# Expert sums closed and added in three regions, the last expert's addition between its halves, 60 of 72 conversion pieces among the experts

## The chip, the cores and the metric

One core of one Trainium2 chip runs the whole program in one launch. The metric is the device time in microseconds (us) of one execution. Engines are named as in the profile: PE (TensorE), DVE (VectorE), ACT (ScalarE), POOL (GpSimd), SP (SyncE, which here only issues DMAs).

## What is computed

Sparse attention over 4 x 576 tokens gives x with 2304 rows of 512. Then two stages follow, cut here to what the change touches:

```python
P = sinkhorn(exp(x @ w_gate - max))            # 2304 x 8
out = 0
for e in range(8):                             # 8 experts, hidden size 1024
    h = np.maximum(x @ w1[e], 0.0)
    out += P[:, e:e + 1] * (h @ w2[e])
xn = out / sqrt(mean(out * out) + 1e-6) * rms_g
g = xn @ w_gate; val = xn @ w_val              # 512 x 1536
return (g / (1 + exp(-g)) * val) @ w_out       # 1536 x 512
```

The weights `w_gate`, `w_val` and `w_out` of the last stage come as 64-bit numbers and are made into 32-bit numbers by integer arithmetic on DVE.

## The kernel before, in words

**Tiling.** The 2304 tokens lie in three thirds `qd` of six tiles of 128. A third is used as a 2 x 2 block matrix: tiles 0 to 2 are the upper half, tiles 3 to 5 the lower (`half`), and the 512 columns are two blocks of 256 (`col`). Every matrix product is taken in a scheme of seven block products instead of eight, and every factor is split into a high and a low part, so that one block product is three matmuls for each of two chunks: `product` (L1151) issues six matmuls of 128x384 into the PSUM buffer `ub`.

**Order of work.** After attention, expert 0 is done in a plain way. Experts 1 to 7 are 42 *groups* n = 0 to 41: for each expert, its hidden half `hh` 0 over the three thirds (0, 1, 2), then half 1 over (2, 1, 0). A group has 14 *slots*; in each, one `product` of the first layer is issued and then one `unit` (L1752, nine matmuls of 128x256 into the PSUM buffer `db`) of the second layer, which belongs to the slot 12 earlier (`LAG`). So the last units of an expert run in the next expert's first group, n = 6k. Every second unit completes one of seven second-layer products k = 0 to 6, and `evict_1(n, k)` takes it from `db` into `acc`, the third's output sums: for k = 0, 2, 3, 4 of hidden half 0 by a copy on ACT (L1773), otherwise by an addition on DVE (L1775, 768 columns, or 1536 for k = 5). First-layer outcomes in `ub` are copied by ACT (L1294), put through a ReLU by ACT (L1298, L1302), or added on DVE (L1183).

**Closing an expert.** After k = 5 and k = 6 of hidden half 1, one half of a third is complete. `weigh` multiplies it by the router's P in place on ACT (three times L1788), and `gather` sends it by an adding DMA of POOL's queue to `y1d` in DRAM (L1796). The next expert begins with the third that the last one ended with, so its copy L1773 must wait until that DMA has read `acc`. For the last expert the DMA goes the other way, `acc += y1d` (L1798), and the normalization of that half waits for it.

**Normalization.** `norm_scale` takes the mean square of a tile (ACT, POOL) and scales it (`xn`, L1393 on DVE). `turn_tile` transposes the tile on PE (L1403) into `db` and multiplies it on DVE by `rms_g` back into `acc`. `norm_blocks` makes the block sums and their high and low parts (L1420 on ACT; L1421 on DVE or, for two thirds of the tokens, on POOL) and stores them to `xnd` in DRAM by SP's queue (L1430, L1454), from where `load_block` (L1083) brings the seven input blocks of a third into `xt` and `xx`. Three blocks are *plain*, four are sums.

**The last stage.** `passes`: three column ranges p, each over the three thirds, n = 0 to 8, and two halves j a pass, written p0.0, p0.1, p1.0 and so on. A half pass has 14 steps, each with one `product` (seven for `w_gate`, seven for `w_val`), and 12 output products of the half pass before are issued between them. p0.0 has the last 12 units of the experts in their place.

**What sets the order.** No scheduler moves instructions: they are issued as the code is run. A `Background` clock `bg` is pumped twice a slot; `bg.add(steps, slots)` spreads steps over pumps, a `Queue` holds steps with lags in pumps, and `drain(tag)` issues at once all that is left of a tag. The 72 *conversion pieces* (`conversion`, seven DVE operations L831 to L855, a load and a store each) are such a queue `conv`; 48 are begun at group 5 and 24 at pass 1, with a lag `CONV_WAIT` ahead of each.

Of the kernel before, what the change touches and what calls it, by code (L numbers as in the profile page):

```python
# [8 lines left out]
F32 = mybir.dt.float32  # L9
F32R = mybir.dt.float32r  # L10
# [103 lines left out]
def kernel(  # L114
# [1262 lines left out]
    def norm_scale(qd, t0):  # L1377

        ss, junk = cv[:, 1280 + t0 : 1283 + t0], cv[:, 768:1280]
# [18 lines left out]
        steps = [(1, lambda t=t: sq(t)) for t in range(3)] + [(1, mean), (0, root)]  # L1398
        return steps + [(2 if t == 0 else 0, lambda t=t: xn(t)) for t in range(3)]
# [10 lines left out]
    def norm_blocks(qd, i, spare, close):  # L1410
# [34 lines left out]
        def part(k):  # L1445
            src = (b12, tb, ta, b21)[k]
            parts(src, highs[k // 2][:, 256 * (k % 2) : 256 * (k % 2 + 1)], src.bitcast(F32R), nc.gpsimd if close else nc.vector)
            return 0 if close else 256
# [10 lines left out]
        steps = [plain, add1, keep, add2] + [lambda k=k: part(k) for k in range(4)] + [keep2]  # L1459
        return [(0.85 if close else 1.2, f) for f in steps]  # L1460


    with tc.manual_schedule():
# [263 lines left out]
        norm = Queue(bg)  # L1727
        turns = {}
# [32 lines left out]
        def evict_1(n, k):  # L1761
# [21 lines left out]
            if hh == 1 and k >= 5:  # L1783
                half = k - 5

                def weigh(m):
                    b = 3 * half + m
                    nc.scalar.activation(  # L1788
                        acc[:, qd, b], acc[:, qd, b], AF.Copy, scale=prob[:, tile_of(qd, b), g : g + 1]
                    )  # L1790

                def gather():
                    t, y = acc[:, qd, 3 * half : 3 * half + 3], y1d[:, qd, half]
                    if g < E - 1:
                        bg.drain("first")
                        nc.gpsimd.dma_start(out=y, in_=t, accum_op=ALU.add)  # L1796
                    else:
                        nc.gpsimd.dma_start(out=t, in_=y, accum_op=ALU.add)  # L1798
                        norm.add([(SUM_WAIT, lambda: None)] + norm_scale(qd, 3 * half), ("scale", qd, half))

                bg.add([lambda m=m: weigh(m) for m in range(3)] + [gather], 4, bg.now + 1, ("expert", qd))

        def turn_tile(qd, t, ps, spare, close):
            bg.drain(("expert", qd))
            norm.drain(("scale", qd, t // 3))
            norm_turn(ps, qd, t)
            if t >= 3:
                norm.add(norm_blocks(qd, t - 3, spare, close), ("blocks", qd))
# [12 lines left out]
        for n in (NGP - 3, NGP - 2):  # L1821
            for at, tiles in TURN_AT:
                turns[14 * n + at] = [(n, t) for t in tiles]
# [10 lines left out]
        def second(slot):  # L1834
# [13 lines left out]
            for m, t in turns.get(slot, ()):  # L1848
                if m not in spares:
                    spares[m] = spare_of(m)  # L1850
                turn_tile(groups[m][2], t, db[5], spares[m], True)
# [23 lines left out]
        halves = {}  # L1875
# [69 lines left out]
        for k in ready:  # L1945
            load_block(nmap[k], *to, k)
# [165 lines left out]
```

## Time and profile before

| what | value |
|---|---|
| time, median of 3 runs | 2287.49 us (2285.51 to 2291.5) |
| profiled execution | 2289.84 us, of which its span is 2288.0 us |
| PE busy | 2066.1 us, 90% of the span |
| DVE busy | 1663.8 us, 73% |
| ACT busy | 1175.6 us, 51% |
| POOL busy | 178.0 us, 8% |
| DMA traffic | 391.20 MB, mean 171 GB/s |

PE is busy nine tenths of the span, and the rest is idle time in certain places. A row of windows gives for a stretch of the span its length and each engine's busy time with its instructions, then the granted TensorE clock as a share of full speed, and the DMA engines' share and rate. A row of waits says which PE work stood still for which operation of which engine or DMA.

### The profile page before, as it was taken

To read this page: it belongs to the slowest core of one execution; us is meant where nothing else is said; L and a number is where in the kernel's file an instruction comes from. 1 tells how busy PE (TensorE), PEld (TensorE's weight loads), DVE (VectorE), ACT (ScalarE), POOL (GpSimd) and SP (SyncE) were. 2 spreads that over 40 slices of the span, in tenths; PEclk is the share of its full clock that TensorE was granted. 3 is DMA by queue.
4 is the path that set the end of the run, shared out by engine and by line. 5 is a ranking of instruction groups with operands and counts; after the bars stand their busy time and mean duration, and the time that the engine had idled before them with its cause. 6 is when DMAs were issued, how large, how long until landed. Compare 5 with 4: busy or idle time off the path is not lost. (4 is left out here: it accounts for less than half of the span.)

```text
span 2288.0 us, 37002 instructions
## 1 busy us (share of the span) xinstructions
PE 2066.1 (90%) x13611; PEld 1961.8 (86%) x13611; DVE 1663.8 (73%) x3553; ACT 1175.6 (51%) x2719; POOL 178.0 (8%) x235
## 2 busy tenths in 40 slices
PE   8999997998999899899989979998985699997698
PEld 7888877998998899899989979997985589986697
DVE  4667548877789688778968877895875766776554
ACT  7766234755556465555646555564654444433222
POOL 6433100000000000000000000000002200000000
PEclk9999999999999899999999999999997799999799
DMA  7687755667356636735663674466347663541241
GB/s 186 185 224 200 225 187 211 211 209 204 125 181 176 195 120 221 196 131 173 182 212 129 197 203 145 157 180 207 134 121 221 166 198 132 173 139 60 99 172 55
DMA packets 305396, 391.20 MB, mean 171 GB/s; under 512 B 78464, under 2 KB 208704, under 8 KB 305216
## 3 DMA queue, kind: packets, MB, share of 16 engines
q1 hardware_dynamic: 298080, 353.52, 47.3%
q0 software_dynamic: 7136, 35.33, 8.1%
q8 instruction: 107, 1.75, 0.3%
q14 instruction: 73, 0.60, 0.1%
HBM read 294.41 MB, written 94.37 MB: 170 GB/s over the span
## 5 line engine op out<-in xcount | busy, mean ns | idle before, releaser
L1151 PE MATMUL ub<-xt,w1t 128*128 128x384 f32 x2328 | 481.8, 344 | 69.4 <-ACT fa L1294 29.8
L1151 PEld LDWEIGHTS ub<-xt,w1t 128*128 128x128 f32 x2328 | 406.5, 194 | 78.3 <-ACT fa L1294 31.8
L1151 PE MATMUL ub<-xx,w1t 128*128 128x384 f32 x1956 | 406.6, 345 | 52.2 <-ACT fa L1294 26.0
L1752 PE MATMUL db<-w2t,ht 128*128 128x256 f32 x2772 | 389.9, 286 | 10.0 <-DVE acc L1775 10.0
L1151 PEld LDWEIGHTS ub<-xx,w1t 128*128 128x128 f32 x1956 | 342.2, 195 | 61.4 <-ACT fa L1294 26.9
L1752 PEld LDWEIGHTS db<-w2t,ht 128*128 128x128 f32 x2772 | 377.0, 194 | 14.1 <-DVE acc L1775 14.1
L1752 PE MATMUL db<-w2t,hx 128*128 128x256 f32 x2520 | 349.6, 283 | 6.1 <-DVE acc L1775 5.8
L1752 PEld LDWEIGHTS db<-w2t,hx 128*128 128x128 f32 x2520 | 333.6, 189 | 15.5 <-DVE acc L1775 14.9
L1183 DVE TENSOR_TENSOR fa<-ub,fa 128x384 f32<-128x384 f32 x360 | 199.4, 554 | 182.7 <-PE ub L1151 169.6
L1302 ACT ACTIVATE fa<-fa 128x384 f32<-128x384 f32 x252 | 132.3, 525 | 289.6 <-DVE fa L1183 289.1
L1775 DVE TENSOR_TENSOR acc<-db,acc 128x768 f32<-128x768 f32 (+1 forms) x210 | 234.0, 1114 | 51.9 <-PE db L1752 49.7
L1179 DVE TENSOR_TENSOR ht<-fa,ht 128x384 fp32r<-128x384 f32 x344 | 189.1, 551 | 91.0 <-ACT ht L1176 90.1
L1179 DVE TENSOR_TENSOR hx<-fa,hx 128x384 fp32r<-128x384 f32 x316 | 174.5, 552 | 52.3 <-ACT hx L1176 51.1
L1176 ACT ACTIVATE ht<-fa 128x384 fp32r<-128x384 f32 x344 | 177.3, 518 | 31.7 <-DVE fa L1354 30.7
L1257 DVE TENSOR_TENSOR fa<-fa 128x384 f32<-128x384 f32 x336 | 186.1, 554 | 6.8 <-ACT fa L1298 3.3
L1176 ACT ACTIVATE hx<-fa 128x384 fp32r<-128x384 f32 x316 | 163.5, 521 | 51.0 <-DVE fa L1354 48.1
L1294 ACT COPY fa<-ub 128x384 f32<-128x384 f32 x252 | 119.3, 473 | 135.7 <-PE ub L1151 132.9
L1796 POOL DMA_DIRECT2D y1d<-acc x36 | 31.2, 868 | 1255.3 <-DVE acc L1775 609.9
L1319 ACT COPY fa<-ub 128x384 f32<-128x384 f32 x108 | 51.6, 478 | 125.4 <-PE ub L1151 125.0
L1773 ACT COPY acc<-db 128x768 f32<-128x768 f32 x84 | 67.3, 801 | 87.7 <-DMA y1d<-acc 65.8
L915 DVE TENSOR_TENSOR w1t<-fa,w1t 128x256 fp32r<-128x256 f32 (+1 forms) x170 | 88.8, 526 | 15.4 <-ACT w1t L912 15.3
L1788 ACT ACTIVATE acc<-acc,prob 128x512 f32<-128x512 f32 x126 | 86.0, 712 | 11.3 <-DVE acc L1775 11.3
(250 smaller groups left out, 3070.4 us busy)
## 6 DMA issues: line engine op xcount, KB each, us to landing
xt<-xdt SPq DMA_DIRECT2D x111, 768.0 KB
xx<-xdt SPq DMA_DIRECT2D x92, 768.0 KB
y1d<-acc POOLq DMA_DIRECT2D x36, 768.0 KB, 9.9
xt<-xnd SPq DMA_DIRECT2D x25, 768.0 KB
xx<-xnd SPq DMA_DIRECT2D x24, 768.0 KB
fa<-in_moe_w_dram SPq DMA_DIRECT2D x56, 256.0 KB
raw<-in_moe_w_dram SPq DMA_DIRECT2D x56, 256.0 KB
xdt<-fa SPq DMA_DIRECT2D x14, 512.0 KB
```

What stands on the lines that cost most here:

```text
L915: nc.vector.tensor_tensor(out=at(7 + k, n), in0=src, in1=at(k, n).bitcast(F32), op=ALU.subtract)
L1151: nc.tensor.matmul(ps[:, :TH], w[i][:, c], x[:, k, c], start=first and c == 0 and n == 0, stop=c == 1 and n == 2, skip_group_check=True,)
L1176: nc.scalar.activation(h[0], src, func)
L1179: engine.tensor_tensor(out=h[1], in0=src, in1=h[0].bitcast(F32), op=ALU.subtract)
L1183: nc.vector.tensor_tensor(out=out, in0=ps, in1=more, op=ALU.add)
L1257: nc.vector.tensor_tensor(**kw)
L1294: nc.scalar.copy(z[nm], ps)
L1302: nc.scalar.activation(z[nm], z[nm], AF.Relu)
L1752: nc.tensor.matmul(spot(k, m), hm[x], w[y], start=BEGIN[k] and r == 0 and m in FIRST[PAIR[k]] and i == 0, stop=r == 1 and i == 2, skip_gro ...
L1773: nc.scalar.copy(a, ps)
L1775: nc.vector.tensor_tensor(out=a, in0=ps, in1=a, op=ALU.add)
L1788: nc.scalar.activation(acc[:, qd, b], acc[:, qd, b], AF.Copy, scale=prob[:, tile_of(qd, b), g : g + 1])
```

## The change

Five things change.

1. **Three regions.** An expert's third is closed in three parts as its products end: after k = 1 (lower half, left columns), after k = 5 (upper half), after k = 6 (lower half, right columns). So there are 18 adding DMAs an expert in place of 12 halves over six of them: per third, two of 384 KB and one of 768 KB. A copy L1773 waits for its own region alone.
2. **The last expert.** Its `acc` is weighed and `y1d` is added to it after hidden half 0; hidden half 1 is then added by SCALAR_TENSOR_TENSOR with P as the scalar, three for each product. The normalization is queued right behind k = 5 and k = 6.
3. **Normalization.** `xn` runs on ACT; all low parts run on DVE; the transposes stand at slots 29 to 34 and 32 to 37 behind their groups in place of 30 to 35; the lags in `norm_blocks` are longer.
4. **Blocks of the first pass.** The three plain blocks are loaded as soon as they are made, the others when a product needs them (`fetch_left`).
5. **Conversion.** 60 pieces begin at group 5 with a lag of 7 pumps, 12 at pass 1 with a lag of 12, in place of 48 with 11 and 24 with 3.

```diff
-    CONV_WAIT = (11, 3)
+    CONV_WAIT = (7, 12)
+    CONV_EP = 60
-    TURN_AT = ((30, (0,)), (31, (1,)), (32, (2,)), (33, (3,)), (34, (4,)), (35, (5,)))
-    SUM_WAIT = 3
+    TURN_AT = (29, 30, 31, 32, 33, 34), (32, 33, 34, 35, 36, 37)
+    BLOCK_LAG = (2.5, 1.6, 0.85)
...
         def xn(t):
-            nc.vector.tensor_scalar(
-                out=a[:, t0 + t], in0=a[:, t0 + t], scalar1=ss[:, t : t + 1], scalar2=None, op0=ALU.mult
-            )
-            return 256
+            nc.scalar.activation(a[:, t0 + t], a[:, t0 + t], AF.Copy, scale=ss[:, t : t + 1])
...
-            parts(src, highs[k // 2][:, 256 * (k % 2) : 256 * (k % 2 + 1)], src.bitcast(F32R), nc.gpsimd if close else nc.vector)
+            parts(src, highs[k // 2][:, 256 * (k % 2) : 256 * (k % 2 + 1)], src.bitcast(F32R))
...
-        steps = [plain, add1, keep, add2] + [lambda k=k: part(k) for k in range(4)] + [keep2]
-        return [(0.85 if close else 1.2, f) for f in steps]
+        steps = [plain, add1, keep], [add2] + [lambda k=k: part(k) for k in range(4)] + [keep2]
+        return [[(BLOCK_LAG[qd], f) for f in x] for x in steps]
...
             if hh == 0 and k in (0, 2, 3, 4):
-                bg.drain(("expert", qd))
+                bg.drain(("expert", qd, half, col if half else None))
                 nc.scalar.copy(a, ps)
+            elif (g, hh) == (E - 1, 1):
+                if k in (0, 2, 3):
+                    bg.drain(("expert", qd, half, col if half else None))
+                for m in range(3):
+                    nc.vector.scalar_tensor_tensor(
+                        out=a[:, m], in0=ps[:, m], scalar=prob[:, tile_of(qd, 3 * half + m), g : g + 1],
+                        in1=a[:, m], op0=ALU.mult, op1=ALU.add,
+                    )
+                    bg.vector(512 if col is None else 256)
...
+            if hh == (g < E - 1) and k in (1, 5, 6):
+                close_region(g, qd, *((1, 0) if k == 1 else (0, None) if k == 5 else (1, 1)))
+            if (g, hh) == (E - 1, 1) and k >= 5:
+                scales[k - 5].add(norm_scale(qd, 3 * (k - 5)), ("scale", qd))
+
+        def close_region(g, qd, half, col):
+            part = slice(0, DM) if col is None else slice(256 * col, 256 * (col + 1))
+
+            def weigh(m):
+                b = 3 * half + m
+                a = acc[:, qd, b, part]
+                nc.scalar.activation(a, a, AF.Copy, scale=prob[:, tile_of(qd, b), g : g + 1])
+
+            def gather():
+                t, y = acc[:, qd, 3 * half : 3 * half + 3, part], y1d[:, qd, half, :, part]
+                bg.drain("first")
+                if g < E - 1:
+                    nc.gpsimd.dma_start(out=y, in_=t, accum_op=ALU.add)
+                else:
+                    nc.gpsimd.dma_start(out=t, in_=y, accum_op=ALU.add)
...
-        norm.drain(("blocks", passes[0][1]))
-        for k in ready:
-            load_block(nmap[k], *to, k)
+        left = [(nmap[k], *to, k) for k in ready]
+
+        def fetch_left(k):
+            for x in list(left):
+                if x[3] == k or made(x[2], x[3]):
+                    norm.drain(("plain" if x[3] < 3 else "blocks", x[2]))
+                    load_block(*x)
+                    left.remove(x)
```

**ACT where expert 3 takes over from expert 2 (groups 12 and 13).** `hx` and `ht` are hidden values, `fa` holds first-layer outcomes, `db_3991` is a product's sum in PSUM, `prob` is P; a name with DMASW is the landing of a DMA of POOL's queue. Before:

```order
L1788 ACTIVATE acc<-acc,prob 128x512
L1053 ACTIVATE w2t<-raw_7708 128x256 [waits PE_49] x2
L1176 ACTIVATE hx<-fa 128x384 [waits Activation_49]
L1302 ACTIVATE fa<-fa 128x384 [waits DVE_49]
L1788 ACTIVATE acc<-acc,prob 128x512 x2
L1176 ACTIVATE hx<-fa 128x384 [waits Activation_49]
L1298 ACTIVATE fa<-ub_4232 128x384 [waits PE_49]
L1788 ACTIVATE acc<-acc,prob 128x512
L1773 COPY acc<-db_3991 128x3x256 [waits DMASW3_49,PE_49,Activation_49]
L1176 ACTIVATE ht<-fa 128x384
L1294 COPY fa<-ub_4231 128x384 [waits PE_49]
L1176 ACTIVATE ht<-fa 128x384
```

And now:

```order
L1803 ACTIVATE acc<-acc,prob 128x512
L1054 ACTIVATE w2t<-raw_7744 128x256 [waits PE_49] x2
L1177 ACTIVATE hx<-fa 128x384 [waits Activation_49]
L1303 ACTIVATE fa<-fa 128x384 [waits DVE_49]
L1803 ACTIVATE acc<-acc,prob 128x256 x2
L1177 ACTIVATE hx<-fa 128x384 [waits Activation_49]
L1299 ACTIVATE fa<-ub_4232 128x384 [waits PE_49]
L1803 ACTIVATE acc<-acc,prob 128x256
L1773 COPY acc<-db_3991 128x3x256 [waits DMASW7_49,PE_49]
L1177 ACTIVATE ht<-fa 128x384 [waits Activation_49]
L1295 COPY fa<-ub_4231 128x384 [waits PE_49]
L1177 ACTIVATE ht<-fa 128x384
```

The three weighings behind k = 6 are now of 256 columns, and the copy L1773 behind them waits for a DMA of another place in POOL's queue: before it was the one that follows these weighings, now it is that of k = 1, which stands ten slots ahead.

**ACT at product 0 of pass 0.** L1319 and L1320 are the copy of the product's `ub` in the kernel before and in the changed one; L1420 and L1419 are the parts of the last block of third 2, with which pass 0 begins; L1383 and L1385 squares; L1395 the scaling `xn`. Before:

```order
L1298 ACTIVATE fa<-ub_4232 128x384
L1788 ACTIVATE acc<-acc,prob 128x512
L1420 ACTIVATE norm_r<-acc 128x512
L1420 ACTIVATE norm_r<-acc 128x256
L1176 ACTIVATE ht<-fa 128x384
L1420 ACTIVATE norm_r<-acc 128x256
L1420 ACTIVATE norm_r<-cv 128x256
L1420 ACTIVATE fa<-cv 128x256
L1420 ACTIVATE fa<-acc 128x256
L1319 COPY fa<-ub_4231 128x384
L1176 ACTIVATE hx<-fa 128x384 x2
L1337 ACTIVATE fa<-fa 128x384
```

And now:

```order
L1177 ACTIVATE hx<-fa 128x384
L1299 ACTIVATE fa<-ub_4232 128x384
L1395 ACTIVATE acc<-acc,cv 128x512 x2
L1177 ACTIVATE ht<-fa 128x384
L1320 COPY fa<-ub_4231 128x384
L1419 ACTIVATE norm_r<-acc 128x256
L1395 ACTIVATE acc<-acc,cv 128x512
L1177 ACTIVATE hx<-fa 128x384
L1419 ACTIVATE norm_r<-cv 128x256
L1177 ACTIVATE hx<-fa 128x384
L1338 ACTIVATE fa<-fa 128x384
L1419 ACTIVATE fa<-cv 128x256
```

The pass's first copy stood behind all six parts of the block; now four of them, those of the block sums, come behind it, with scalings of third 1 among them.

**DVE in pass 6.** `cv` is the conversion's buffer, L831 and L832 the first of a piece's seven operations, L918 and L919 differences for the weights of the next column range, L915 and L916 their low parts. Before:

```order
L831 TENSOR_SCALAR cv<-cv 128x256
L832 TENSOR_SCALAR cv<-cv 128x256
L838 TENSOR_SCALAR cv<-cv 128x256
L842 SCALAR_TENSOR_TENSOR cv<-cv 128x256
L848 TENSOR_SCALAR cv<-cv 128x256
L849 SCALAR_TENSOR_TENSOR cv<-cv 128x256
L855 TENSOR_TENSOR cv<-cv 128x256
L831 TENSOR_SCALAR cv<-cv 128x256
L832 TENSOR_SCALAR cv<-cv 128x256
L838 TENSOR_SCALAR cv<-cv 128x256
L842 SCALAR_TENSOR_TENSOR cv<-cv 128x256
L848 TENSOR_SCALAR cv<-cv 128x256
```

And now:

```order
L832 TENSOR_SCALAR cv<-cv 128x256
L833 TENSOR_SCALAR cv<-cv 128x256
L919 TENSOR_TENSOR fa<-fa 128x256
L839 TENSOR_SCALAR cv<-cv 128x256
L843 SCALAR_TENSOR_TENSOR cv<-cv 128x256
L916 TENSOR_TENSOR w2t<-fa,w2t 128x512
L849 TENSOR_SCALAR cv<-cv 128x256
L850 SCALAR_TENSOR_TENSOR cv<-cv 128x256
L916 TENSOR_TENSOR xt<-fa,w2t 128x256
L856 TENSOR_TENSOR cv<-cv 128x256
L1184 TENSOR_TENSOR fa<-ub_4231,fa 128x384
```

The pieces stood back to back, since what was left of the queue was issued at once where a weight needed it; now the operations of a piece stand between others.

## Rows read from the trace of the kernel before

**Rows 1.** Waits of PE in the whole span: us in total, times, longest.

```profile
PE ub L1151 <- ACT fa L1294: 55.8, 7, 9.7
PE ub L1151 <- DVE fa L1183: 37.0, 22, 8.8
```

**Rows 2.** Windows of groups 18, 20 and 21 (fourth of the seven experts).

```profile
926.13:963.64 37.51, 32.21 (x213) 31.28 (x212) 35.23 (x79) 22.74 (x54) 1.73 (x2) 0.95 0.76 222
...
1002.94:1032.82 29.88, 29.88 (x213) 29.56 (x212) 25.54 (x55) 17.86 (x37) 0.00 (x0) 1.00 0.32 104
1032.82:1065.02 32.20, 30.68 (x213) 29.75 (x212) 29.43 (x68) 22.20 (x52) 0.00 (x0) 1.00 0.49 171
```

**Rows 3.** Windows of group 41, the first pass's halves, a later half, pass 6.

```profile
1686.20:1749.56 63.36, 36.33 (x237) 34.99 (x235) 42.06 (x80) 30.83 (x74) 14.16 (x17) 0.85 0.61 152
1749.56:1797.87 48.31, 35.81 (x216) 34.90 (x217) 36.43 (x69) 22.98 (x55) 8.54 (x10) 0.85 0.59 187
1797.87:1846.07 48.20, 34.12 (x145) 29.85 (x146) 32.50 (x66) 21.90 (x53) 7.02 (x8) 0.75 0.68 199
1920.90:1943.90 23.00, 23.00 (x121) 21.37 (x120) 17.97 (x45) 9.54 (x22) 0.00 (x0) 1.00 0.22 69
2089.30:2137.30 48.00, 30.39 (x121) 27.08 (x121) 29.83 (x69) 11.01 (x23) 0.00 (x0) 0.79 0.25 80
2137.30:2177.30 40.00, 28.97 (x122) 26.21 (x121) 23.12 (x56) 9.30 (x20) 0.00 (x0) 0.83 0.38 131
```

**Rows 4.** Waits of PE from 1686 to 1874 us (whole list has ten rows).

```profile
PE db L1403 <- DVE acc L1393: 17.7, 5, 4.9
PE ub L1151 <- DMA xt<-xnd: 17.5, 1, 17.5
...
PE ub L1151 <- ACT fa L1298: 4.4, 1, 4.4
...
PE ub L1151 <- DVE w2t L915: 0.3, 1, 0.3
```

**Rows 5.** Timeline of ACT at the boundary of two experts.

```profile
761.93 0.71 ACT L1788 ACTIVATE acc<-acc,prob 128x512 f32<-128x512 f32 x1
774.42 0.80 ACT L1773 COPY acc<-db 128x768 f32<-128x768 f32 x1 [11.78 <-DMA y1d<-acc]
```

**Rows 6.** Windows of the six groups that open experts 2 to 7.

```profile
562.33:603.25 40.92, 32.05 (x212) 31.53 (x211) 20.24 (x40) 16.67 (x34) 0.86 (x1) 0.87 0.62 191
...
sum 243.62, PE 191.79 PEld 188.66 DVE 122.67 ACT 98.00 POOL 5.17; mean PE 31.97 PEld 31.44 DVE 20.44 ACT 16.33 POOL 0.86
```

**Rows 7.** DMA issues from 762 to 765 us: KB, us to landing.

```profile
y1d<-acc POOLq DMA_DIRECT2D x1, 768.0 KB, 11.4
```

**Rows 8.** Groups of instructions by form: busy us, mean ns of one.

```profile
L1775 DVE TENSOR_TENSOR acc<-db,acc 128x768 f32<-128x768 f32 x168 | 160.2, 954 | 23.6 <-PE db L1752 21.8
...
L760 DVE SCALAR_TENSOR_TENSOR ht<-psh,ht 128x256 fp32r<-128x256 f32 x56 | 23.5, 420 | 37.5 <-ACT ht L759 37.5
...
L1393 DVE TENSOR_SCALAR acc<-acc,cv 128x512 f32<-128x512 f32 x18 | 7.6, 481 | 3.9 <-POOL cv L1390 3.9
...
L1421 DVE TENSOR_TENSOR acc<-acc 128x256 fp32r<-128x256 f32 x14 | 5.7, 419 | 0.1
```

**Rows 9.** Timeline of DVE at one conversion piece in pass 6.

```profile
2100.28 0.29 DVE L831 TENSOR_SCALAR cv<-cv 128x256 uint32<-128x256 uint32 x1 [2.71 <-DMA cv<-in_moe_w_out_dram]
...
2102.87 0.55 DVE L1183 TENSOR_TENSOR fa<-ub,fa 128x384 f32<-128x384 f32 x1
```

**Rows 10.** Timeline of SP's queue: stores and the load of normalized blocks.

```profile
1734.04 2.84 SPq L1430 DMA_DIRECT2D xnd<-norm_r  x2
...
1744.33 2.95 SPq L1083 DMA_DIRECT2D xt<-xnd  x4
```

**Rows 11.** Timeline of PE at the start of pass 0.

```profile
1749.56 2.29 PE L1151 MATMUL ub<-xt,w1t 128*128 128x384 f32 x6 [17.49 <-DMA xt<-xnd]
...
1755.94 1.21 PE L1151 MATMUL ub<-xt,w1t 128*128 128x384 f32 x6
```

More of the change, by code (lines that the diff above doesn't have):

```diff
@@ L1377, in norm_scale @@
     def norm_scale(qd, t0):
[L1379 removed]
+        ss = cv[:, 1280 + 6 * qd + t0 : 1283 + 6 * qd + t0]
+        junk = xt_flat[:, 7680:8192] if qd else cv[:, :512]
         a = acc[:, qd]
@@ L1782, in evict_1 @@
                     prepare_2(E, (0, 2, 1, 3)[k - 3])
[L1783 to L1801, printed above, removed]
@@ L1803, in turn_tile @@
-        def turn_tile(qd, t, ps, spare, close):
-            bg.drain(("expert", qd))
-            norm.drain(("scale", qd, t // 3))
+            if hh == (g < E - 1) and k in (1, 5, 6):
[15 more added lines that the diff above has]
+                    nc.gpsimd.dma_start(out=t, in_=y, accum_op=ALU.add)
+            bg.add(
+                [lambda m=m: weigh(m) for m in range(3)] + [gather], 4, bg.now + 1, ("expert", qd, half, col)
+            )
@@ L1806, in turn_tile @@
+        def turn_tile(qd, t, ps, spare):
+            scales[t // 3].drain(("scale", qd))
             norm_turn(ps, qd, t)
             if t >= 3:
-                norm.add(norm_blocks(qd, t - 3, spare, close), ("blocks", qd))
+                plain, more = norm_blocks(qd, t - 3, spare)
+                norm.follow(plain, ("plain", qd))
+                norm.follow(more, ("blocks", qd))
         def spare_of(n):
@@ L1874, with made @@
         nmap, nfree = xmap, free
-        halves = {}
+        fs = [2 * NG + i for i in (0, 2, 1, 3)]
+        conv_items = [(nm, f, half) for f in range(2 * NG) for nm in "gvo" for half in range(2)]
+        conv_items += [(nm, f, half) for two in (fs[:2], fs[2:]) for nm in "gv" for f in two for half in range(2)]
+        conv_items += [("o", f, half) for f in fs for half in range(2)]
+        def made(qd, k):
+            return not any(x[0] == ("plain" if k < 3 else "blocks", qd) for x in norm.items)
         for n, (g, hh, qd) in enumerate(groups):
@@ L1898 @@
                 bg.drain("first")
-                items = [(nm, f, half) for f in range(2 * NG) for nm in "gvo" for half in range(2)]
-                conversion(items, CONV_WAIT[0])
+                conversion(conv_items[:CONV_EP], CONV_WAIT[0])
             if ends and n < NGP - 1:
@@ L1933 @@
                             ready.append(PROD[i + 2][1])
-                        if not to[0] or (r, i) >= (1, 1) and not any(x[0] == ("blocks", to[1]) for x in norm.items):
-                            for k in ready:
+                        for k in list(ready):
+                            if not to[0] or (r, i) >= (1, 0) and made(to[1], k):
                                 bg.later(1, lambda s=nmap[k], k=k, to=to: load_block(s, *to, k), "x")
-                            ready = []
+                                ready.remove(k)
                     if ends and i in PARTS_AT:
@@ L1989, in evict @@
             if p == 0:
-                for q in range(NQD):
-                    norm.drain(("blocks", q))
+                for x in (qd, qd - 1):
+                    norm.drain(("blocks", x))
                 nc.scalar.copy(a, db[b])
@@ L2013 @@
             if n == 1:
-                fs = [2 * NG + i for i in (0, 2, 1, 3)]
-                items = [(nm, f, half) for two in (fs[:2], fs[2:]) for nm in "gv" for f in two for half in range(2)]
-                items += [("o", f, half) for f in fs for half in range(2)]
-                conversion(items, CONV_WAIT[1])
+                conversion(conv_items[CONV_EP:], CONV_WAIT[1])
             for j in range(NG // 2):
-                if j and p == 0 and more:
-                    norm.drain(("blocks", qd2))
                 gs, hs = {}, {}
@@ L2031 @@
                 fresh = more and j == NG // 2 - 1
-                if fresh:
+                if fresh and p:
                     k = PROD[0][1]
@@ L2040 @@
                     use = hidden_v(gs, hs, (n, j)) if ci else hidden_g(gs, (n, j))
+                    if fresh and p == 0 and ci == 1:
+                        norm.drain(("blocks", qd2))
+                        k = PROD[0][1]
+                        load_block(nmap[k], True, qd2, k)
                     for i, (wk, xk, which, begins) in enumerate(PROD):
+                        if first_round and ci == 0:
+                            fetch_left(xk)
                         if i == 1 and ci == 1:
```

24 lines of the change are left out of this document (12 added, 12 removed).

## The prediction

> **What bounds the kernel now.** I read the page first: PE is busy 90% of the span of 2288.0 us, so something short of a tenth can be won where it stands still, or where it runs at the lower clock. The list of PE's waits says for what it stands still: mostly for first-layer outcomes, 55.8 us in only seven waits on ACT's copy L1294, and 37.0 us on DVE's L1183 [rows 1]. Seven waits of up to 9.7 us are one event that comes back, not a general lack of ACT. So I cut the span by groups, from the first product of one to that of the next, and looked at windows. A group with nothing in its way takes 29.88 us at clock 1.00; a group with DVE busy 35.23 or 29.43 us takes 37.51 or 32.20 [rows 2]. Three kinds of places take longer.
>
> *The groups that open an expert.* On ACT's timeline a last weighing ends at 762.6, and the copy L1773 behind it starts at 774.42, after 11.78 us in which it waited for the adding DMA to `y1d` [rows 5]. The copies of `ub` stand behind it on ACT, and PE stops. The six groups take 243.62 us together [rows 6], six undisturbed ones 6 x 29.88 = 179.3: **64.3 us** too many.
>
> *The passage to the last stage.* Group 41, p0.0 and p0.1 take 63.36, 48.31 and 48.20 us, 159.9 together [rows 3]. Undisturbed, the group would be 29.88. A half pass is 23.00 [rows 3]. For p0.0, 14 products and 12 units, where a group has 14 and 14 of the same number of columns, I estimate 29.88 x 26/28 = 27.7. So 79.3 us are too many. PE's waits from there on are ten rows that sum to 56.1 us, among them 17.7 for `xn` (L1393), 17.5 for the load of `xnd`, 4.4 for a ReLU in L1298 [rows 4]. PE's busy time is 36.33 + 35.81 + 34.12 = 106.3 us, 25.7 above the 80.6 of undisturbed work: the transposes, and matmuls at the lower clock. The granted clock is 0.85, 0.85 and 0.75 [rows 3]; the first six matmuls after the wait of 17.49 us take 2.29 us, and six of the same kind 6 us later 1.21 [rows 11]: the lower of its two levels (1.2 and 2.4 GHz) after it stood still. I put 13 of the 25.7 to transposes and 12.4 to slow running.
>
> *Pass 6.* Its halves take 48.00 and 40.00 us, with clock 0.79 and 0.83 [rows 3], against 46.0 for two quiet ones; with the transfer of the last weights I allow 47, so **41 us** too many. What stands there on DVE are conversion pieces, issued all at once and each behind its load: 2.71 us of idle time, then seven operations from 2100.28 to 2102.87 [rows 9].
>
> **The change part by part.** The sum is made against the profiled execution, span 2288.0 and 1.84 around it, 2289.84; it lies 2.35 above the median.
>
> *A, the three regions.* A copy L1773 now waits for a DMA that stands ten slots ahead (k = 0) or six (k = 2, 3). Six slots are 6 x 29.88/14 = 12.8 us. The adding DMA of 768 KB takes 11.4 us to land in the same stretch [rows 7], and with 0.9 us for its issue it is 12.3: in time, barely. I leave 4 us over the six experts for the cases in which it is late, and take **-60**. The trace shows no DMA of 384 KB of this kind. At best the copies never wait: -64.3. At worst a region cut to rows of half the length takes twice as long for its bytes, as long as two: 22.8 + 0.9 - 12.8 = 10.9 us, nearly the old wait, and A is 0. I take the first since the region has half the bytes. The weighings are 9 of 256 or 512 columns in place of 6 of 512, on an ACT that is busy 51%.
>
> The Trainium skill speaks against cutting a DMA: its page "DMA: Bandwidth & Descriptors", section "Anatomy of one DMA — SWDGE (gpsimd) path", puts a fixed cost of about 2.0 us ahead of the bytes, so each cut pays it again; by its figures an estimate for 768 KB is 3.8 us and for 384 KB 2.9, and the sum would have A at -64.3. The trace does not agree on the length: 11.4 us for 768 KB.
>
> *B, twelve more conversion pieces among the experts.* A piece is 2.59 us of DVE from first to last operation [rows 9], so 31.1 us go into some 30 groups, 1.0 a group. Where DVE has room this costs nothing: the cover is PE's own 29.88 us, beside which DVE had 25.54 without loss [rows 2]. Where it is full, at 35.23 in 37.51 and 29.43 in 32.20, it is added to the time. Of the six groups of an expert I count two and a half as full, so 31.1 x 2.5/6 = **+13**. Bounds: 0 if all find room, +31 if none does.
>
> *C, the passage.* What goes: the waits for `xn`, which came late because the sum's DMA stood ahead of it, 17.7, and the wait of 4.4 in L1298 behind it; with a share of the slow running, 12.4 x 22.1/56.1 = 4.9. That is -27. What comes: `xn` is ACT's (18 x 0.481 = 8.7 us leave DVE), 24 low parts come to DVE from POOL at 0.42 (10), and 21 additions become 3 operations each; by 3 x 0.420 against 0.954 that is 0.3 more each, 6 [rows 8]. DVE has 7.5 us more in a stretch where it is waited for; half of it exposed, +4. The wait of 17.5 for the `xnd` blocks splits: the three plain blocks come at product 0, the sums at product 2. But the sums' parts now stand behind the copy of product 0 on ACT, as the order of ACT shows, and then five stores and a load must pass SP's queue, where a store is 0.5 to 2.8 us and a load 2.95 [rows 10]. I work out 9 us at product 0 and 10 at product 2, so +1.5, and +2 for the clock after a second stop. C is **-20**. Bounds: 0 if the second stop is as long as the first was; -40 if the plain blocks are ready in time and only the second is left.
>
> *D, pass 6.* Twelve pieces in place of 24 are spread from p2 on with a lag of 12, and the order shows the last ones between other operations. I leave 3 of the 41 us: **-38**. If one forced run of pieces stays at the end, it is -28; if nothing is left, -41.
>
> Sum: -60 + 13 - 20 - 38 = -105, 2184.8 for a profiled execution, and 2182 for the median.
>
> **The rivals.**
> *The passage gains nothing* (C = 0): the second stop takes what `xn` gives. For it: 17.49 us was the longest wait of all [rows 11], and the blocks still pass ACT, DVE and SP in turn. Against: the waits for `xn` have nothing left to wait for. 2182 + 20 = 2202.
> *DVE shows all moved pieces* (B = +31): 2182 + 18 = 2200. For it: two groups in six are already longer for DVE's sake. Against: 29.88 at 25.54 busy.
> *More than hoped* (C = -40, B = +6): 2155.
> *The cut regions land late* (A = 0): 2242. For it: rows of half the length; against: half the bytes, at ten slots' notice for k = 0.
> *DVE becomes what bounds the experts*, slower than before. With a lag of 7 in place of 11 the pieces come denser, and each stands ahead of L1183, for which PE already waits 37.0 us [rows 1]. If all 60 were exposed, 60 x 2.59 = 155 us against -118 for A, C and D: 2287.5 + 37 = 2325. It decides once 118/155 = 76% of them are. Against it: group 20 had one and a half on average and lost nothing [rows 2].
>
> **How the numbers follow.** My forecast 0.55, within 2166 to 2198 (A to -64 or -52, B 5 to 20); the passage gains nothing 0.17; all moved pieces shown 0.13; more than hoped 0.08; late regions 0.04; DVE the bound 0.03. The range from 2155 to 2222 holds the first four at their centres, with some room beyond 2202 for two of them in part together. A measurement of this kernel can tell 0.3%, some 7 us, from no change. All cases but the last are faster by more than that: faster 0.95, same 0.02, slower 0.03.
>
> **What would show it.** A: no wait of ACT's copy L1773 on `y1d<-acc` over 2 us, and groups 6k+1 of 30 us, at clock 1.00. B: groups of the experts' inner stretch some 1 us longer where DVE was above 28 us, else the same. C: no wait of PE for `xn` in the transposes, two stops at products 0 and 2 of p0.0, and the three windows at 140 us. D: p6.0 and p6.1 at 50 us together, and no row of idle DVE behind a load of `w_out`. I am wrong if an adding DMA of 384 KB lands after 13 us or more, if the list of PE's waits has more on L1183 than 37 us, or if a wait on `xnd` above 17 us stands at either product.

## The result, and the profile after

The changed kernel takes **2172.44 us** (median of 4 runs, 2169.7 to 2174.41), the kernel before 2289.29 beside it (2285.51 to 2291.5): a ratio of 0.949, 95% interval 0.9472 to 0.9508. The forecast was 2182, between 2155 and 2222. The span of the profiled execution is 2167.6 us, 120.4 less than before; the sum had 105.

The stages, cut at the first product of a group or half pass, in windows (columns as in [rows 2]). First one of the groups that open an expert (n = 6k + 1) and the sum of all six, then groups 18 and 21, group 41, the halves p0.0, p0.1, p6.0 and p6.1, and last groups 6 to 40 as one window:

```profile
558.52:588.38 29.86, 29.86 (x213) 29.54 (x211) 21.86 (x47) 16.07 (x33) 1.28 (x1) 1.00 0.80 254
...
sum 179.93, PE 179.15 PEld 177.24 DVE 127.56 ACT 100.48 POOL 9.86; mean PE 29.86 PEld 29.54 DVE 21.26 ACT 16.75 POOL 1.64
...
903.00:938.90 35.90, 32.35 (x213) 31.28 (x212) 35.33 (x80) 23.48 (x56) 3.45 (x3) 0.95 0.82 228
999.64:1031.80 32.16, 30.90 (x212) 29.77 (x211) 31.46 (x75) 22.31 (x52) 0.00 (x0) 1.00 0.61 213
1625.08:1673.12 48.04, 35.55 (x236) 34.38 (x234) 42.42 (x99) 28.62 (x68) 2.90 (x3) 0.90 0.40 116
1673.12:1723.36 50.24, 34.76 (x216) 33.87 (x216) 33.20 (x74) 21.23 (x50) 0.85 (x1) 0.84 0.46 157
1723.36:1764.22 40.86, 33.26 (x144) 29.29 (x145) 31.33 (x71) 20.92 (x48) 0.85 (x1) 0.82 0.72 219
2007.50:2032.90 25.40, 23.25 (x121) 21.23 (x121) 20.42 (x44) 10.49 (x23) 0.00 (x0) 1.00 0.29 88
2032.90:2057.30 24.40, 23.26 (x121) 21.30 (x120) 18.05 (x42) 9.42 (x21) 0.00 (x0) 1.00 0.38 136
...
523.44:1625.08 1101.64, 1062.91 (x7353) 1044.06 (x7352) 959.56 (x2046) 685.27 (x1520) 67.86 (x59) 0.99 0.65 191
```

The opening groups take 179.93 us together in place of 243.62 [rows 6]: each is within 0.6 us of an undisturbed one, at clock 1.00. Group 18 has DVE's busy time of before and is 1.6 us shorter, group 21 has two us more of it and the same length [rows 2]. The passage (group 41, p0.0, p0.1) takes 139.1 us in place of 159.9, pass 6 takes 49.8 in place of 88.0 [rows 3]. All of groups 6 to 40 take 1101.64; the same stretch of before, 525.89 to 1686.20, is 1160.31. Without the opening groups these are 921.7 and 916.7: 5.0 us more.

| term | forecast | profile |
|---|---|---|
| A, six opening groups | -60 | -63.7 |
| B, the other groups from 6 to 40 | +13 | +5.0 |
| C, passage | -20 | -20.7 |
| D, pass 6 | -38 | -38.2 |
| all other stages | 0 | -2.8 |

The last line holds the stretch up to group 6, which differs from run to run: in kernels that are the same up to group 4 it ended between 522 and 530 us. Differences of spans below 8 us are therefore read from windows here, not from the span.

What PE waits for in the passage, the first four rows and the last of nine, which sum to 38.7 us where ten summed to 56.1 [rows 4]:

```profile
PE ub L1152 <- DMA xt<-xnd: 15.7, 2, 9.9
PE db L1402 <- DVE acc L1403: 5.6, 4, 3.4
PE ub L1152 <- ACT last_r L913: 5.1, 1, 5.1
PE db L1752 <- DVE acc L1778: 4.3, 1, 4.3
...
PE db L725 <- ACT acc L2019: 0.7, 1, 0.7
```

No row of `xn` (now L1395) is left, nor of the ReLU (L1298, now L1299). The wait on `xnd` is now two, 5.8 and 9.9 us. The pages' lists of DMA issues give the adding DMAs with their median time to landing, before:

```profile
y1d<-acc POOLq DMA_DIRECT2D x36, 768.0 KB, 9.9
```

And after:

```profile
y1d<-acc POOLq DMA_DIRECT2D x36, 384.0 KB, 6.4
y1d<-acc POOLq DMA_DIRECT2D x18, 768.0 KB, 9.3
```

These are the experts 1 to 6: nine adding DMAs an expert in place of six. The first point of the section on the change has 18 and 12; the lists decide.

### The profile page after: what moved, and what is told of

Read it like the earlier page. It is cut to its first block, busy times and chain, and to the rows that moved or that the text cites. A ratio compares the mean times of both kernels' runs of the same rounds, so it can differ in the third digit from the quotient of the medians.

```text
span 2167.6 us, 37111 instructions
## 1 busy us (share of the span) xinstructions
PE 2040.1 (94%) x13611; PEld 1939.6 (89%) x13611; DVE 1661.7 (77%) x3601; ACT 1199.1 (55%) x2800; POOL 194.8 (9%) x232
## 5 line engine op out<-in xcount | busy, mean ns | idle before, releaser
L1152 PEld LDWEIGHTS ub<-xt,w1t 128*128 128x128 f32 x2328 | 401.2, 192 | 45.3 <-DVE fa L1184 18.4
L1152 PE MATMUL ub<-xx,w1t 128*128 128x384 f32 x1956 | 396.9, 340 | 14.3 <-DVE fa L1184 11.2
L1752 PE MATMUL db<-w2t,ht 128*128 128x256 f32 x2772 | 382.6, 283 | 7.6 <-DVE acc L1784 6.9
L1752 PEld LDWEIGHTS db<-w2t,ht 128*128 128x128 f32 x2772 | 369.5, 190 | 11.8 <-DVE acc L1784 10.8
L1152 PEld LDWEIGHTS ub<-xx,w1t 128*128 128x128 f32 x1956 | 334.9, 191 | 21.3 <-DVE fa L1184 13.6
L1184 DVE TENSOR_TENSOR fa<-ub,fa 128x384 f32<-128x384 f32 x360 | 199.4, 554 | 164.3 <-PE ub L1152 147.9
L1784 DVE TENSOR_TENSOR acc<-db,acc 128x768 f32<-128x768 f32 (+1 forms) x189 | 211.5, 1119 | 41.2 <-PE db L1752 39.9
L1177 ACT ACTIVATE ht<-fa 128x384 fp32r<-128x384 f32 x344 | 177.3, 517 | 32.0 <-DVE fa L1355 31.1
L1809 POOL DMA_DIRECT2D y1d<-acc x54 | 62.3, 1154 | 1173.1 <-ACT acc L1803 698.8
L1320 ACT COPY fa<-ub 128x384 f32<-128x384 f32 x108 | 51.6, 478 | 109.9 <-PE ub L1152 109.8
L1803 ACT ACTIVATE acc<-acc,prob 128x256 f32<-128x256 f32 (+1 forms) x189 | 102.5, 572 | 11.9 <-DVE acc L1784 11.7
L916 DVE TENSOR_TENSOR w1t<-fa,w1t 128x256 fp32r<-128x256 f32 (+1 forms) x170 | 88.5, 524 | 10.3 <-ACT w1t L913 10.2
L913 ACT ACTIVATE w1t<-fa 128x256 fp32r<-128x256 f32 (+1 forms) x170 | 80.6, 495 | 2.1 <-DVE fa L919 2.1
```

Of the source, the lines that this page charges most:

```text
L913: nc.scalar.activation(at(k, n), src, AF.Copy)
L916: nc.vector.tensor_tensor(out=at(7 + k, n), in0=src, in1=at(k, n).bitcast(F32), op=ALU.subtract)
L1152: nc.tensor.matmul(ps[:, :TH], w[i][:, c], x[:, k, c], start=first and c == 0 and n == 0, stop=c == 1 and n == 2, skip_group_check=True,)
L1177: nc.scalar.activation(h[0], src, func)
L1184: nc.vector.tensor_tensor(out=out, in0=ps, in1=more, op=ALU.add)
L1752: nc.tensor.matmul(spot(k, m), hm[x], w[y], start=BEGIN[k] and r == 0 and m in FIRST[PAIR[k]] and i == 0, stop=r == 1 and i == 2, skip_gro ...
```

## The experiments

Each edit is made in the changed kernel unless it says otherwise. Times are medians beside the kernel before on the same chip.

**e1, two halves again.**

```diff
-            if hh == (g < E - 1) and k in (1, 5, 6):
-                close_region(g, qd, *((1, 0) if k == 1 else (0, None) if k == 5 else (1, 1)))
+            if hh == (g < E - 1) and k >= 5:
+                close_region(g, qd, k - 5, None)
...
-                bg.drain(("expert", qd, half, col if half else None))
+                bg.drain(("expert", qd, half, None))
```

> The changed kernel, but every expert's third is closed in two halves again, behind k = 5 and k = 6. Theory (the copies no longer wait for the adding DMA): the six groups that open an expert go back from 179.9 us together to about 243, ACT's copy waits some 11 us in each for y1d, and the time is 2172 + 63 = 2235. Rival (the gain of these groups comes with the other edits, and two halves would do): they stay below 190 and the time is below 2182.

2245.49 us, ratio 0.9819 (0.9775 to 0.9863). The opening groups, first and sum, and ACT's waits on the adding DMA:

```profile
563.38:603.38 40.00, 32.90 (x212) 32.38 (x211) 21.61 (x47) 16.25 (x33) 0.86 (x1) 0.87 0.63 197
...
sum 239.66, PE 191.77 PEld 188.64 DVE 127.26 ACT 100.75 POOL 6.06; mean PE 31.96 PEld 31.44 DVE 21.21 ACT 16.79 POOL 1.01
```

```profile
ACT acc L1773 <- DMA y1d<-acc: 61.3, 6, 12.0
```

As the theory has it, and by itself as large as A: six waits of up to 12.0 us, 59.7 us more. The edit closes the last expert in halves too, and there group 40 is 41.10 us in place of 30.52: a seventh stop, in which DVE's addition (L1778) waits 11.5 us for `acc<-y1d`. That makes the 10 us beyond the expectation.

**e2, the DMA later in the program.**

```diff
-            bg.add(
-                [lambda m=m: weigh(m) for m in range(3)] + [gather], 4, bg.now + 1, ("expert", qd, half, col)
-            )
+            tag = ("expert", qd, half, col)
+            bg.add([lambda m=m: weigh(m) for m in range(3)], 3, bg.now + 1, tag)
+            bg.add([gather], 1, bg.now + (10 if g < E - 1 else 4), tag)
```

> The changed kernel, with each region's adding DMA of experts 1 to 6 issued three slots (6.4 us) later. Theory (six slots hold the landing barely; the smallest spare times of the copies behind it are 1.0 to 4.4 us in the trace): the copies of k = 2 and k = 3 wait 2 to 5 us, PE stops 0 to 3.3 us each time, and the six opening groups are 5 to 25 us longer together, time about 2184. Rival (the DMA lands sooner when it does not run beside another, so there is room): the groups stay within 2 us of 179.9, time 2172.

2173.66 us, opening groups 179.96. This tells nothing of the spare time: the DMA started as early as ever, at the first boundary 11.97 us behind the first product of group 6 (540.72 - 528.75, where the changed kernel has 535.41 - 523.44). Nothing else stands in POOL's queue there, so the DMA goes when the weighings are done, wherever its line is.

**e3, the conversion split of before.**

```diff
-    CONV_WAIT = (7, 12)
-    CONV_EP = 60
+    CONV_WAIT = (11, 3)
+    CONV_EP = 48
```

> The changed kernel with the conversion split as before: 48 pieces among the experts with a lag of 11, 24 from pass 1 on with a lag of 3. Theory (pass 6 was long because of forced pieces, and twelve pieces cost the experts some 5 us): pass 6 goes from 49.8 to 88 us, groups 6 to 40 get 5 us shorter, time 2205. Rival 1 (twelve pieces cost 13, as forecast): groups 13 shorter, time 2197. Rival 2 (pass 6 gained from the other edits): pass 6 stays near 50, time 2167 to 2172.

2209.86 us, ratio 0.9663 (0.962 to 0.9706). Windows of p6.0 and p6.1, then of groups 6 to 40:

```profile
2003.41:2056.29 52.88, 30.07 (x122) 26.72 (x122) 32.31 (x77) 11.01 (x23) 0.00 (x0) 0.74 0.26 80
2056.29:2096.23 39.94, 28.77 (x122) 26.05 (x121) 23.09 (x56) 9.30 (x20) 0.00 (x0) 0.83 0.38 131
...
522.35:1618.20 1095.85, 1061.71 (x7352) 1043.86 (x7351) 938.84 (x1966) 684.60 (x1520) 67.85 (x59) 0.99 0.65 187
```

Pass 6 is back at 92.8 us at a clock of 0.74 and 0.83, so D is the pieces alone. Groups 6 to 40 are 5.8 us shorter: that is the price of the added pieces, eleven of which run in this window (58 in place of 47), the theory's 5 and not rival 1's 13.

**e4, the pieces' arithmetic left out** (six of seven operations of the 60 pieces, so these weights of the last stage are not converted).

```diff
+            if len(items) == CONV_EP:
+                head = number = tail = lambda: 0
             conv.add([(wait, head), (STEP, number), (STEP, tail)], tag)
```

> The changed kernel without the first six of the seven DVE operations of the 60 conversion pieces among the experts; so the weights of the last stage are not right. It takes about 60 x 2.2 = 132 us of work from DVE. Theory (a piece costs time only in the groups n = 6k and 6k+3, where DVE is full, 20 of the 60, and there some 0.6 of its length): groups 6 to 40 get 20 to 30 us shorter, time about 2147. Rival (five twelfths of every piece are exposed, as forecast): 55 us shorter, time 2117. DVE as the bound of all groups would give 132.

2142.06 us, ratio 0.9367 (0.9325 to 0.9409). Groups 6 to 40 in one window:

```profile
528.13:1599.04 1070.91, 1054.11 (x7352) 1037.59 (x7351) 867.44 (x1695) 685.17 (x1520) 67.85 (x59) 1.00 0.67 196
```

DVE is busy 92.1 us less than in the changed kernel, and the time is 30.7 less: a third of the work taken away was exposed. Of the 30.7, the windows of groups 6k give 14.5 and those of 6k+3 12.3, all others 3.9. The place was right; but even there DVE's work is not exposed in full.

**e5, block sums ahead of product 0.**

```diff
+            if left and k == PROD[0][1]:
+                norm.drain(("blocks", left[0][2]))
```

> The changed kernel, with all steps of the last block of third 2 (block sums, their parts, stores) issued ahead of product 0 of pass 0, behind the loads of the plain blocks. Theory (the second stop is there because four parts stand behind the copy of product 0 on ACT): the wait of 9.9 us at product 2 falls to 0 to 3, that of 5.8 at product 0 stays, p0.0 is about 43 us in place of 50, time 2165. Rival (stores and load through SP's queue are what takes the time): the wait at product 2 stays above 8, time 2172.

2167.75 us, ratio 0.9473 (0.945 to 0.9495). The waits on the `xnd` blocks:

```profile
PE ub L1152 <- DMA xt<-xnd: 10.3, 3, 5.2
```

p0.0 is 45.27 us in place of 50.24. The wait at product 2 is 4.9 in place of 9.9, that at product 0 stays (5.2). So about half of the second stop was that these steps stood behind the copy of product 0. That the other half is the stores and the load is not shown by this run; e12 takes most of it out with the same stores and loads. Between theory and rival.

**e6, all blocks loaded together.**

```diff
-                        if first_round and ci == 0:
-                            fetch_left(xk)
+                        if first_round and (ci, i) == (0, 0) and left:
+                            norm.drain(("blocks", left[0][2]))
+                            for x in left:
+                                load_block(*x)
+                            left.clear()
```

(and no plain block earlier than the others).

> The changed kernel, with the seven blocks of the first pass loaded together behind the last block's steps, as before. Theory (splitting the load bought nothing by itself, since it makes two stops of one): one stop of 14 to 17 us at product 0, none at product 2, time 2169 to 2174. Rival (the split is worth a product's time or more): the stop is above 20 us and the time above 2178.

2163.34 us, ratio 0.9449 (0.9427 to 0.947):

```profile
PE ub L1152 <- DMA xt<-xnd: 10.8, 1, 10.8
```

One stop of 10.8 us, shorter than the theory had it, and the passage is 135.7 us in place of 139.1: faster than the change. The split as the change has it does not pay. The windows of the passage give 3.4 of the 9.1 us between the medians; where the rest comes from is open.

**e7, the last expert's addition behind its second half** (plain additions on DVE, weighing, `acc += y1d`, then the normalization).

```diff
-            elif (g, hh) == (E - 1, 1):
+            elif False:
...
-            if hh == (g < E - 1) and k in (1, 5, 6):
+            if hh == 1 and k in (1, 5, 6):
...
                     nc.gpsimd.dma_start(out=t, in_=y, accum_op=ALU.add)
+                    if col != 0:
+                        scales[half].add([(3, lambda: None)] + norm_scale(qd, 3 * half), ("scale", qd))
...
```

> The changed kernel, with the last expert weighed and added behind its hidden half 1, as before (in three regions), its evictions as plain additions, and the normalization behind that DMA. Theory (the 22 us that went from the passage were waits behind this DMA): group 41 to p0.1 take 155 to 162 us in place of 139, time about 2192. Rival (the waits go into the stops at the xnd loads, which get shorter by as much): within 4 us of 139, time 2172.

2198.92 us, ratio 0.9605 (0.9585 to 0.9625). The first two rows of PE's waits in the passage:

```profile
PE ub L1152 <- DMA xt<-xnd: 19.9, 2, 10.3
PE db L1402 <- ACT acc L1395: 16.2, 4, 8.9
```

The waits for `xn` (L1395 here) are back with 16.2 us, those on `xnd` grow by 4.2, and the passage takes 166.5 us, 27.4 more. The theory holds; the expectation's upper end was 162.

**e8, the scalings `xn` on DVE.**

```diff
-            nc.scalar.activation(a[:, t0 + t], a[:, t0 + t], AF.Copy, scale=ss[:, t : t + 1])
+            nc.vector.tensor_scalar(
+                out=a[:, t0 + t], in0=a[:, t0 + t], scalar1=ss[:, t : t + 1], scalar2=None, op0=ALU.mult
+            )
+            return 256
```

> The changed kernel with the 18 scalings xn on DVE again. Theory (DVE is waited for in half of the passage): 8.7 us of work more there, half of it exposed, 2176. Rival (neither engine bounds there; loads and stores do): 2171 to 2174, with the three windows within 1.5 us of 139.

2184.64 us, ratio 0.9548 (0.9526 to 0.957): longer than either forecast. The passage is 140.7 us, 1.6 more, which is nearly the rival's; in e2 to e4, which leave the passage as it is, it took 138.6 to 140.2. The rest stands in pass 6, 60.7 us in place of 49.8. DVE's timeline there, the end of one piece and the start of the next:

```profile
2054.67 0.42 DVE L856 TENSOR_TENSOR cv<-cv 128x256 f32<-128x256 f32 x1
2057.74 0.29 DVE L832 TENSOR_SCALAR cv<-cv 128x256 uint32<-128x256 uint32 x1 [2.65 <-DMA cv<-in_moe_w_out_dram]
```

Two pieces stand back to back again, the second behind its own load. The first of the twelve late pieces ends in p3.0 in place of p2.1, and three in place of two are left for p6.1. The background clock, which holds the conversion back while it counts DVE as full, was told of 18 operations more; that this is what delays the pieces is likely and not shown.

**e9, e6 and a shorter lag.**

```diff
-    BLOCK_LAG = (2.5, 1.6, 0.85)
+    BLOCK_LAG = (2.5, 1.6, 0.45)
```

> The kernel with the seven blocks loaded together (e6), and the lag of the block steps of third 2 cut from 0.85 to 0.45 pumps, so that two of them are issued a pump and the last block's steps stand some four slots earlier. Theory (the one stop of 10.8 us is there because DVE issues the last block's parts 6 us too late, by the lag and not for want of time): the stop is 2 to 6 us and the time 2156 to 2160. Rival (DVE is full in group 41 and the parts only push out what PE needs there): group 41 is longer by what the stop is shorter, time 2163.

**2156.3 us**, ratio 0.9414 (0.9398 to 0.943), the fastest kernel here. Group 41, p0.0, p0.1:

```profile
1626.05:1672.47 46.42, 37.43 (x237) 36.47 (x235) 41.41 (x97) 29.90 (x72) 1.88 (x2) 0.89 0.56 167
1672.47:1710.64 38.17, 30.92 (x217) 29.95 (x217) 34.07 (x77) 20.13 (x48) 1.87 (x2) 0.99 0.42 149
1710.64:1751.84 41.20, 32.93 (x144) 28.75 (x145) 31.42 (x71) 20.94 (x48) 0.85 (x1) 0.84 0.71 218
```

Of PE's waits on `xnd` 0.2 us are left, none of it in the passage. Group 41 is not longer for it but 7.2 us shorter than in e6, and p0.0 runs at a clock of 0.99. DVE had the time; the queue's spacing had made the block sums late.

**e10, e6 with all 72 pieces among the experts** (`CONV_WAIT` 5, `CONV_EP` 72).

> The kernel of e6 with all 72 conversion pieces among the experts (lag 5) and none in the passes: the cost of twelve more pieces there, doubled. Theory (twelve pieces cost the experts about 5 us, and passes 2 to 6 lose some 4 us of pieces): groups 6 to 40 are 4 to 8 us longer, passes 2 to 6 some 4 shorter, time 2163 to 2167. Rival (the room of DVE is used up by the 60 and more pieces are exposed in full): groups 15 to 31 longer, time 2175 to 2190.

2175.85 us, ratio 0.9499 (0.9483 to 0.9515). Groups 6 to 40, here and in e6:

```profile
529.53:1640.41 1110.88, 1061.30 (x7353) 1041.22 (x7352) 982.49 (x2127) 683.13 (x1520) 67.86 (x59) 1.00 0.66 193
```

```profile
523.35:1624.34 1100.99, 1061.60 (x7352) 1042.35 (x7351) 959.25 (x2046) 684.84 (x1520) 67.86 (x59) 0.99 0.66 191
```

9.9 us more for 23.2 us more of DVE, a share of 0.43. Passes 2 to 6 are 3.5 us shorter (237.8 and 241.3, from the same cuts). Of the 12.5 us in all 4.7 more stand in group 5, where the pieces begin (34.75 in place of 30.09): with the lag of 5 DVE waits for the load of a piece.

```profile
DVE cv L832 <- DMA cv<-in_moe_w_gate_dram: 4.1, 1, 4.1
```

The time is the rival's, the share lies between theory and rival: the second twelve cost nearly twice the first twelve in groups 6 to 40.

**e11, low parts on POOL, and the weighings later.**

```diff
+            parts(src, highs[k // 2][:, 256 * (k % 2) : 256 * (k % 2 + 1)], src.bitcast(F32R), nc.gpsimd if qd else nc.vector)
...
-                [lambda m=m: weigh(m) for m in range(3)] + [gather], 4, bg.now + 1, ("expert", qd, half, col)
+                [lambda m=m: weigh(m) for m in range(3)] + [gather], 4, bg.now + (7 if g < E - 1 else 1),
```

> Two edits in the changed kernel that lie in stages far apart, each read by its own windows. In the passage, the low parts of the sums of two thirds are on POOL again: if DVE's work is half exposed there, as forecast, the three windows are some 4 us shorter than 139.2; if not, within 1.5 of it, or longer since a part on POOL takes 0.87 us in place of 0.42. At the boundaries of experts, the weighings themselves, and so the adding DMAs, come three slots later (in e2 only the DMA's place in the program moved): by the spare times of 1.0 to 4.4 us the copies of k = 2 and k = 3 should now wait 2 to 5 us, and the six opening groups be 5 to 25 us longer together; if the landings get shorter as they shift, they stay within 2 us of 179.9.

2177.63 us, ratio 0.9506 (0.9487 to 0.9525). Opening groups, one and the sum, and ACT's waits on the adding DMA:

```profile
754.07:790.02 35.95, 31.40 (x213) 30.88 (x211) 22.01 (x46) 18.15 (x38) 2.18 (x2) 0.95 0.74 220
...
sum 189.53, PE 181.40 PEld 178.68 DVE 127.31 ACT 113.07 POOL 15.27; mean PE 30.23 PEld 29.78 DVE 21.22 ACT 18.85 POOL 2.54
```

```profile
ACT acc L1773 <- DMA y1d<-acc: 20.8, 8, 7.0
```

Three slots later, ACT waits 20.8 us in eight waits and the six groups lose 9.6: the spare time is there but not three slots of it. The passage is 141.2 us, 2.1 longer than with the parts on DVE; a part takes 0.75 to 0.93 us on POOL and 0.42 on DVE, so this does not price DVE's work by itself.

**e12, the shorter lag alone.**

> The changed kernel with one number changed: the lag of the block steps of third 2, 0.45 pumps in place of 0.85, with the loads split as the change has them. Theory (late block sums were the whole fault, and loading plain blocks ahead of the others costs nothing once they are all made in time): both waits on xnd together below 3 us, the three windows of the passage within 1 us of the 125.8 of e9, time 2153 to 2160. Rival (the split loads are themselves late, in SP's order): a wait of 4 us or more stays at product 2, windows above 130.

2157.14 us, ratio 0.9425 (0.9396 to 0.9455); the passage is 125.9 us, and of the waits on `xnd` there remains

```profile
PE ub L1152 <- DMA xt<-xnd: 1.9, 1, 1.9
```

As the theory has it: with the sums made in time, it does not matter whether the loads are split.

## Why the prediction came out as it did

The range held and the time lay 9.6 us below the value: A, B and the other stages came out below their terms, together 15 us below the sum in the profiled execution, which is the fastest of the four. By its own steps:

**A was right in mechanism and nearly in size.** e1 gives it alone. The margin was called bare, 12.3 us in 12.8, and 4 us were left for late landings; there were none. Between landing and copy the changed kernel has 1.0 to 6.0 us for the copies of k = 2 and k = 3, over 16 for k = 0, and e11 shows that three slots (6.4 us) later is too late. The 12.3 had the issue twice: a landing is counted from the start of the issue, here the one of [rows 7], and 762.93 + 11.4 is where the copy behind it starts, 774.42 [rows 5].

```profile
762.93 0.86 POOL L1796 DMA_DIRECT2D y1d<-acc  x1 [3.28 <-DVE fa L1257]
```

Nor does the bound "A is 0" follow from its words: twice as long for half the bytes would be 11.4 us, not 22.8. The page "DMA: Bandwidth & Descriptors" of the Trainium skill (section "Anatomy of one DMA — SWDGE (gpsimd) path") has the fixed cost from which the prediction estimated 3.8 us for 768 KB and 2.9 for 384. The trace does not agree on the lengths, 9.3 and 6.4 us at the median; and whether a cut pays a fixed cost again cannot be read here, since at the boundaries each DMA of 768 KB ran beside one of 384.

**B is the term that was mis-sized: 5 us, not 13.** Both of its factors were too large. The pieces added to groups 6 to 40 are eleven, and by e3 they add 20.7 us to DVE's busy time there (938.84 to 959.56), not 31.1. And the failing step was "of the six groups of an expert I count two and a half as full", with DVE's work added to the time in full there: 5.8 of the 20.7 us are exposed, 0.28 in place of 0.42. (Against the kernel before it is 5.0 of 25.3, 934.2 to 959.6, with the other edits in the difference.) By e4 the places are groups 6k and 6k+3, and over all groups a third of the pieces' work is exposed. It is not an even share of each group either. Of the 5.8 us 3.9 lie in group 15 alone, here in e3 and in the changed kernel:

```profile
809.15:840.40 31.25, 30.65 (x212) 29.73 (x211) 28.88 (x66) 22.12 (x52) 0.00 (x0) 1.00 0.50 179
```

```profile
806.81:841.93 35.12, 31.69 (x212) 31.16 (x211) 31.20 (x73) 22.44 (x52) 0.00 (x0) 0.95 0.46 153
```

There 2.3 us more of DVE come with one wait of PE on L1184 of 2.4 us and a clock of 0.95. Groups 18 and 21, which the working had as full, lost nothing, against the sign that was named for B. So a piece costs time where it falls into a stretch of DVE without room, and is hidden beside it.

**C came out at -20.7 for -20, with its parts off; that the sum fits so well is luck.** What goes is shown by e7: 27.4 us lie on the last expert's addition, where the working had 27; but 4.2 of them are waits on `xnd`, which the working did not count there. What comes was 3.5 for the split load, 4 for DVE. The load's two stops came (5.8 and 9.9 for 9 and 10). But DVE's 7.5 us more did not come: its busy time in the three windows is 107.0 us, and was 111.0 [rows 3]. And its work is not half exposed: with `xn` back on DVE, 6.6 us more of its busy time, the passage is 1.6 us longer (e8). PE's waits on DVE other than those for `xn` rose from 10.5 to 16.1 us all the same, so that DVE costs nothing there is not shown. The working took it that DVE bounds there because PE waits for it, but the 17.7 us of these waits came from the sum's DMA ahead of `xn`, as the working says itself. What does cost is that the block sums are issued late: e12 takes 13 us out of the passage by one number, and e9 by the same number 10 us beyond e6. The working prices the second stop, but took this spacing as given.

**D was right**, -38.2 for -38, and e3 shows it to be the pieces alone. No wait of DVE for a load of `w_out` is left. It is fragile: e8, which moves nothing in pass 6, lost 10.9 us of it again.

Of the rivals, the one that ended on the other side, DVE as the bound of the experts, is ruled out by e4: all the pieces' arithmetic together costs 30.7 us, where it needed 118. PE's waits on L1184, which it would have raised above 37.0 us [rows 1], fell over the whole span, though in groups 6 to 40 alone they went from 21.3 to 23.3:

```profile
PE ub L1152 <- DVE fa L1184: 26.1, 20, 3.7
```

"All moved pieces shown" is ruled out by e3, late cut regions by the landings, and "the passage gains nothing" by the windows and e7.

How the second stop comes about is to be seen in the changed kernel. PE's timeline at products 0 and 2 of p0.0, the six matmuls after the first wait taking 2.29 us as in [rows 11]:

```profile
1673.14 2.29 PE L1152 MATMUL ub<-xt,w1t 128*128 128x384 f32 x6 [5.77 <-DMA xt<-xnd]
...
1689.14 1.30 PE L1152 MATMUL ub<-xt,w1t 128*128 128x384 f32 x3 [9.88 <-DMA xt<-xnd]
```

ACT's, the copy of product 0 and the first part behind it:

```profile
1675.47 0.48 ACT L1320 COPY fa<-ub 128x384 f32<-128x384 f32 x1 [7.28 <-PE ub L1152]
1675.84 0.42 ACT L1419 ACTIVATE norm_r<-acc 128x256 fp32r<-128x256 f32 x1
```

SP's queue, the load of the plain blocks, the first and the last store of the sums, and their load:

```profile
1668.84 0.87 SPq L1084 DMA_DIRECT2D xt<-xnd  x2
...
1677.62 0.37 SPq L1453 DMA_DIRECT2D xnd<-norm_r  x1
...
1682.57 0.50 SPq L1453 DMA_DIRECT2D xnd<-acc  x1
1684.73 0.87 SPq L1084 DMA_DIRECT2D xt<-xnd  x2
```

The part starts when the copy has run, 1.8 us later the first store of sums starts, at 1682.57 the last, at 1684.73 the load, and PE goes on at 1689.14: the whole chain begins with a product that itself waited. e12 shows that it need not: with the steps issued earlier one wait of 1.9 us is left.

## What to carry to other kernels

Look at a buffer that is reused at a stage boundary by its parts: close each where its last product ends, and give the transfer the slots that lie between it and the part's next writer, since a wait in an engine's queue stops also what stands behind it. A busy share near full does not say that an engine bounds a stage: take work away from it or add some, and look (e4, e8), before pricing it at its full length. Background work wants a rate at which nothing is left to be forced at its due time (e3), and steps on the way to the next stage's input want little spacing: 0.45 pumps in place of 0.85 were worth 13 us here (e12).

## What the runs showed of the hardware

A DMA of 384 KB that adds to DRAM landed in 5.0 to 5.8 us where no other adding DMA ran beside it (the first of the three at each of the six boundaries); the other two, of 768 and 384 KB and issued 4 us apart, took 6.6 to 11.5 us each. Moving a DMA's line in the program did nothing as long as its queue was otherwise empty (e2).

Some operations of DVE took longer while POOL computed. In the passage of the kernel before, with the low parts on POOL, one `fa<-fa` took 1.38 us beside such a part, and another of the same shape 0.55 without:

```profile
1728.71 0.98 POOL L1421 TENSOR_TENSOR cv<-cv,fa 128x256 fp32r<-128x256 f32 x1
1728.74 1.38 DVE L1257 TENSOR_TENSOR fa<-fa 128x384 f32<-128x384 f32 x1
...
1734.71 0.55 DVE L1257 TENSOR_TENSOR fa<-fa 128x384 f32<-128x384 f32 x1
```

In the changed kernel's passage none of that shape takes over 0.56. In e11 24 parts of 0.42 us leave DVE for POOL, 10 us, and DVE's busy time there falls by 3.1 (to 103.8). So moving work from DVE to POOL freed less of DVE than the work's own length.
